# A fused attention and MLP block with its backward pass: k and v projected first with late q tiles, a deeper skew in attention backward, and reordered weight-gradient stages

One core of a Trainium2 chip. The metric is the device time of one execution in microseconds (us).

## The reference

Sequence 2048, width 640, 32 heads of 20, MLP width 1728, bfloat16. Forward: a layer norm, linear attention and a residual, then a layer norm, a gated MLP and a residual. The kernel returns the output and the gradients of x and of the five weights.

```python
def _A_ref(x, wqkv, wo):                     # linear attention
    q, k, v = ...                            # x @ wqkv, split into heads
    phi = lambda t: jnp.where(t > 0, t + 1, jnp.exp(t)) + 1e-6
    pq, pk = phi(q), phi(k)
    kv = jnp.einsum("bhsd,bhse->bhde", pk, v)
    z = jnp.einsum("bhsd->bhd", pk)
    num = jnp.einsum("bhqd,bhde->bhqe", pq, kv)
    den = jnp.einsum("bhqd,bhd->bhq", pq, z)[..., None] + 1e-6
    return merge(num / den) @ wo             # "merge" stands for the transpose and reshape

def _B_ref(x, w1, w3, w2):
    return (_silu(x @ w1) * (x @ w3)) @ w2   # written with einsum in the original

h = x + _A_ref(_layernorm(x), A_wqkv, A_wo)
h2 = h + _B_ref(_layernorm(h), B_w1, B_w3, B_w2)
# outputs: h2, and jax.vjp's gradients of x, wqkv, wo, w1, w3, w2 for grad_out
```

All q tiles need only x. But num and den need the sum of pk and v over the whole sequence, so no attention output can begin before the last k and v tile.

## The kernel before

Rows are cut into 16 tiles of 128 (`ST`) and four chunks of four tiles (`SC`, `TPC`); `part()` below issues the next nine of a turn's 54 ghn matmuls (or a piece of the gradient of wo, once those are done). `T`, `V`, `A`, `G` are TensorE, VectorE, ScalarE and GpSimd. In the traces shown here each engine's work comes in the order in which this program lists it. The stages, in order:

1. Projection: for every tile q, then k, then v.

```python
for t in range(ST):
    q = p1_mm(t, 0)                       # ten 320-column matmuls
    if t + 2 < ST:
        p1_norm(t + 2)
    phi(q, pqc[g][:, i, :])
    if t + 1 < ST:
        p1_tr(t + 1)
    k = p1_mm(t, D)
    phi(k, pkc[g][:, i, :])
    v = p1_mm(t, 2 * D)
    A.copy(...)                           # v to va
    ...                                   # statistics, kv_group once per four tiles, stores, loads
```

2. The first four attention outputs, as a chain of steps per tile: `f2_nd` (numerator and denominator), `f2_o` (division), `f2_ot` (transpose), `f2_at` (times wo, plus the residual), `f2_hn` (norm), `f2_ht` (transpose). Products of w2 for the MLP's backward (`filler`) fill TensorE between the steps.

3. Four MLP chunks of 14 column blocks. Per block: the ghh product (backward, with w2; in the first chunk the filler has made it before), gate and up products on TensorE, activations on ScalarE, seven elementwise operations on VectorE. The attention steps of the next chunk ("side steps") come after a whole block:

```python
for fc in range(FT):
    mlp(c, fc, ghh0[:, fc, :] if c == 0 else None)   # gate, up, then 7 elementwise operations
    if o2:
        next(o2)                                     # output products of the chunk before
    if c + 1 < SC:
        for f, i in sorted(side.get(fc, ()), key=lambda x: x[1]):
            f((c + 1) * TPC + i)
```

4. The last output products, the gradient of w2 (its operand hb is hh loaded transposed; grad_out is loaded after the fourth chunk).

5. Attention backward, one turn per tile. The layer-norm backward is one piece, and gnd (the gradient of num and den) is made and transposed within one turn:

```python
def ln_bwd(acc, t, nrm, st, out, res, pl):
    A.activation(out=gs, in_=acc, ..., accum_out=s[:, 0:1])
    V.scalar_tensor_tensor(out=wb[:], ...)
    V.tensor_scalar(...); V.tensor_scalar(...)
    V.scalar_tensor_tensor(out=wb[:], ...)
    A.activation(out=y[:], in_=wb[:], ...)            # waits for VectorE's wb
    V.tensor_tensor(out=out, in0=y[:], in1=res, op=ALU.add)   # out is g_h, waits for ScalarE's y

for t in range(ST + 2):
    g = b_ghn(t) if t < ST else wog       # 54 matmuls in six parts, then b_ln
    u = t - 2
    ...
    part()
    if u >= 0:
        b_go(u)                           # ten matmuls (h), then gnd on VectorE
    part()
    part()
    if u >= 0:
        b_gndT(u)                         # six transposes of gnd
    part()
    if u >= 0:
        b_gkv(u)
        b_gpq(u)
    part()
    if 0 <= t - 1 < ST:
        b_gT(t - 1)                       # transposes of g_h, copy ghT on ScalarE
    part()
```

6. The k and v backward with w1 and w3 gradient products ("jobs", from the transposed block gb) as filler, the x-gradient loop with the rest of them, and last the gradient of wqkv.

Of the kernel before, what the change touches and what calls it, by code (L numbers as in the profile page):

```python
# [8 lines left out]
P = 128  # L9
# [53 lines left out]
def kernel(  # L63
# [86 lines left out]

    p1 = pool("p1", "right")
    ps = pool("p1p", space=PSUM)
    wqkv = p1.tile([P, DT, 3 * D], BF16, name="wqkv")
    wq_v = A_wqkv.rearrange("(c p) n -> p c n", p=P)
    dma(out=wqkv[:, :, 0:D], in_=wq_v[:, :, 0:D])
    dma(out=x_sb[:, 2:4, :], in_=xS[:, 2:4, :])
    dma(out=wqkv[:, :, D:2 * D], in_=wq_v[:, :, D:2 * D])
    dma(out=wqkv[:, :, 2 * D:], in_=wq_v[:, :, 2 * D:])
    for t in range(4, ST, 4):
        dma(out=x_sb[:, t:t + 4, :], in_=xS[:, t:t + 4, :])  # L160
# [3 lines left out]
    def make_mask():  # L164
# [8 lines left out]
        G.memset(kvbd[:], 0.0)  # L173
# [4 lines left out]
    w2 = U1.tile([P, FT, D], BF16, name="w2", tag="D")  # L178
# [18 lines left out]
    pkc, pqc = {}, {}  # L197
    xnT, xns = {}, {}
# [5 lines left out]
    def p1_tr(t):  # L204
        xn = xns.pop(t)
        tr = ps.tile([P, DT, P], BF16, name="tr", bufs=2)
        for c in range(DT):
            T.transpose(tr[:, c, :], xn[:, c * P:(c + 1) * P], ident[:])
        xnT[t] = p1.tile([P, DT, P], BF16, name="xnT", bufs=2)
        A.copy(out=xnT[t][:], in_=tr[:])  # L210

    def p1_mm(t, n0):
        acc = ps.tile([P, 2, 512], F32, name="big", bufs=3)
        for j in range(2):
            for c in range(DT):
                T.matmul(acc[:, j, 0:HD], lhsT=xnT[t][:, c, :],  # L216
                         rhs=wqkv[:, c, n0 + j * HD:n0 + (j + 1) * HD], start=(c == 0), stop=(c == DT - 1))
        return acc

    def phi(acc, dst):  # L220
        mq = p1.tile([P, D], BF16, name="mq", bufs=3)
        A.activation(mq[:].rearrange("p (j n) -> p j n", j=2), acc[:, :, 0:HD], AF.Exp)
        V.tensor_scalar(out=mq[:], in0=mq[:], scalar1=1.0, scalar2=1e-6, op0=ALU.min, op1=ALU.add)
        V.scalar_tensor_tensor(out=dst.rearrange("p (j n) -> p j n", j=2), in0=acc[:, :, 0:HD], scalar=0.0,  # L224
                               in1=mq[:].rearrange("p (j n) -> p j n", j=2), op0=ALU.max, op1=ALU.add)
# [43 lines left out]
    for t in range(ST):  # L269
        g, i = divmod(t, TPC)  # L270
        if i == 0:
            pqc[g] = p1.tile([P, TPC, D], BF16, name="pqc", bufs=2)
            pkc[g] = p1.tile([P, TPC, D], BF16, name="pkc", bufs=2)
        q = p1_mm(t, 0)
        if t + 2 < ST:
            p1_norm(t + 2)
        phi(q, pqc[g][:, i, :])
        if t + 1 < ST:
            p1_tr(t + 1)
        k = p1_mm(t, D)  # L280
        phi(k, pkc[g][:, i, :])
        v = p1_mm(t, 2 * D)
        A.copy(out=va[g % 2][:, i, 0:C].rearrange("p (j h e) -> p j h e", j=2, e=DA)[:, :, :, 0:DH],
               in_=v[:, :, 0:HD].rearrange("p j (h e) -> p j h e", e=DH))
        if t % 2 == 0 and t + 4 < ST:
# [3 lines left out]
        if i == TPC - 1:  # L289
            sl = slice(g * TPC, (g + 1) * TPC)  # L290
            dma(out=pq_v[:, sl, :], in_=pqc[g][:])
            dma(out=pk_v[:, sl, :], in_=pkc[g][:])
            dma(out=va_v[:, sl, :], in_=va[g % 2][:])
            if g < 2:
                load_pqT(g)
# [4 lines left out]
    p1.release()  # L300
# [4 lines left out]
    pa = pool("pa", "right")  # L305
# [10 lines left out]
    def f2_o(t):  # L316
        o_t = pa.tile([P, D], BF16, name="o_t", bufs=2)
        den = pa.tile([P, H], F32, name="den", bufs=2)
# [12 lines left out]
    def f2_ot(t):  # L331
# [3 lines left out]
        oT[t] = pa.tile([P, DT, P], BF16, name="oT", bufs=2)  # L335
        A.copy(out=oT[t][:], in_=tr[:])

    def f2_at(t, tag="nd"):
        for j in range(2):
            at = ps.tile([P, 512], F32, name="at", tag=tag, bufs=2)  # L340
            for c in range(DT):
                T.matmul(at[:, 0:HD], lhsT=oT[t][:, c, :], rhs=wo[:, c, j * HD:(j + 1) * HD],  # L342
                         start=(c == 0), stop=(c == DT - 1))
            xs = x_sb[:, t, j * HD:(j + 1) * HD]
            V.tensor_tensor(out=xs, in0=at[:, 0:HD], in1=xs, op=ALU.add)
        ln2.run(x_sb, t, t + 1)

    def f2_hn(t):
        hn[t] = pa.tile([P, D], BF16, name="hn", bufs=2)
# [3 lines left out]
    def f2_ht(t):  # L353
        c, i = divmod(t, TPC)
        if i == 0:
            hnT[c] = pa.tile([P, DT, W], BF16, name="hnT", bufs=2)
# [15 lines left out]
    def mlp(c, fc, ghh):  # L372
        if ghh is None:
            ghp = mm5(w2T, fc, g2T[c])
            ghh = ew("ghh")
            A.copy(out=ghh[:], in_=ghp[:])  # L376
            ghh = ghh[:]
# [4 lines left out]
        A.copy(out=gate[:], in_=gp[:])  # L382
        upp = mm5(w3, fc, hnT[c])
# [8 lines left out]
        V.tensor_tensor(out=gate[:], in0=gate[:], in1=ghh, op=ALU.mult)  # L392
        dma(out=gg_d[F + f0:F + f0 + n, cs], in_=gate[:n, :])
        V.tensor_tensor(out=sig[:], in0=sig[:], in1=up[:], op=ALU.mult)
        V.tensor_tensor(out=sig[:], in0=sig[:], in1=ghh, op=ALU.mult)
        dma(out=gg_d[f0:f0 + n, cs], in_=sig[:n, :])

    def o2_steps(c, q=dma):
# [3 lines left out]
        for n, (i, j, fc) in enumerate(jobs):  # L402
            if fc == 0:
                o2["ps"] = ps.tile([P, 512], F32, name="o2", bufs=2)
                if j == 0:
                    o2["sb"] = pa.tile([P, D], BF16, name="h2", bufs=3)
# [11 lines left out]

    ghh0 = pa.tile([P, FT, W], BF16, name="hhT", bufs=2)
    fill = list(range(FT))  # L420

    def filler(n):
        for _ in range(n):
            if fill:
                fc = fill.pop(0)
                acc = mm5(w2T, fc, g2T[0])
                A.copy(out=ghh0[:, fc, :], in_=acc[:])

# [7 lines left out]
    for step in (2, (f2_ndo, 0), 2, (f2_ot, 0), (f2_ndo, 1), 1, (f2_at0, 0), 1, (f2_ot, 1), (f2_ndo, 2), 1,  # L436
                 (f2_hn, 0), (f2_at0, 1), 1, (f2_ht, 0), (f2_ot, 2), (f2_ndo, 3), 1, (f2_hn, 1), (f2_at0, 2), 1,
                 (f2_ht, 1), (f2_ot, 3), 1, (f2_hn, 2), (f2_at0, 3), 2, (f2_ht, 2), (f2_hn, 3), 1, (f2_ht, 3)):
        if isinstance(step, int):
            filler(step)  # L440
        else:
            step[0](step[1])
    filler(len(fill))

    V.memset(w2[64:, FT - 1, :], 0.0)
    side = {}
    for i in range(TPC):
        for k, fs in ((3 * i, (f2_nd, f2_o)), (3 * i + 1, (f2_ot,)), (3 * i + 2, (f2_at,)),
                      (3 * i + 3, (f2_hn,)), (3 * i + 4, (f2_ht,))):
            side.setdefault(k, []).extend((f, i) for f in fs)  # L450

    for c in range(SC):
        hhT[c] = pa.tile([P, FT, W], BF16, name="hhT", bufs=2)
        o2 = o2_steps(c - 1) if c > 0 else None
        for fc in range(FT):
            mlp(c, fc, ghh0[:, fc, :] if c == 0 else None)
            if o2:
                next(o2)
            if c + 1 < SC:
                for f, i in sorted(side.get(fc, ()), key=lambda x: x[1]):  # L460
                    f((c + 1) * TPC + i)
# [5 lines left out]
            if fc == 5 and c + 2 < SC:  # L467
                load_pqT(c + 2)


    g2 = U1.tile([P, ST, D], BF16, name="g2", tag="Q")
    dma(out=g2[:], in_=goS)
# [10 lines left out]
    pa.release()  # L483
    ps.release()
# [6 lines left out]
    woT = U1.tile([P, DT, D], BF16, name="woT", tag="W6")  # L491
    tail = br.tile([P, DT, P], BF16, name="w13tail")

    def load_w13():
# [4 lines left out]
        dmaT(out=woT[:], in_=A_wo[:, :])  # L499
# [13 lines left out]
    for fc in range(FT):  # L513
# [14 lines left out]
        if fc == 7:  # L528
            load_gg(0)
            load_gg(1)  # L530
# [34 lines left out]
    hnb, pqb, ghT, gnd, gndT = {}, {}, {}, {}, {}  # L565

    def b_load(t):
# [3 lines left out]
        pqb[t] = br.tile([P, D], BF16, name="pqb", bufs=4)  # L571
# [17 lines left out]
    def ln_bwd(acc, t, nrm, st, out, res, pl):  # L589
# [12 lines left out]
        y = pl.tile([P, D], BF16, name="y")  # L602
        A.activation(out=y[:], in_=wb[:], func=AF.Identity, bias=s[:, 3:4], scale=st.rs[:, t:t + 1])  # L603
        V.tensor_tensor(out=out, in0=y[:], in1=res, op=ALU.add)

    def b_ln(acc, t):
        ln_bwd(acc, t, hnb[t][:], ln2, g_h[:, t, :], g2[:, t, :], br)
# [8 lines left out]
    gnd_s = [br.tile([P, CP], BF16, name=f"gnd{i}") for i in range(3)]  # L616
# [3 lines left out]
    def b_go(t):  # L620
        gnd[t] = gnd_s[t % 3]
# [44 lines left out]
    def wo_job(m):  # L666
        acc = ps.tile([P, 2, 512], F32, name="gwo", tag="ghn", bufs=2)
        for j in range(2):
            for t in range(ST):
                T.matmul(acc[:, j, 0:HD], lhsT=o_sb[:, t, m * P:(m + 1) * P], rhs=g_h[:, t, j * HD:(j + 1) * HD],  # L670
                         start=(t == 0), stop=(t == ST - 1))
                if t % 8 == 7:
                    yield
# [11 lines left out]
    for t in range(ST + 2):  # L685
# [4 lines left out]
        u = t - 2  # L690
        if t + 2 < ST:
            b_load(t + 2)
# [214 lines left out]
```

## Time and profile before

| | before |
|---|---|
| time, median (range) | 1003.67 us (999.65 to 1006.38), 3 runs |
| span of the profiled run | 1005.6 us |
| TensorE busy / idle | 902.2 / 103.4 us |
| mean granted clock | 0.976 |

The prediction shows the page's head and the waits. What follows is another cut of the same run, by stage, with borders at the same instruction in both kernels (within 0.2 us), so that the rows can be set against those of the changed kernel. They are: the last projection work to the first gate product; the first chunk; the last output products and the w2 gradient; attention backward; the rest. Columns are window, length, busy us of TensorE, its weight loads, VectorE, ScalarE and GpSimd (instructions in brackets), granted clock, DMA share, GB/s.

```profile
88.05:119.89 31.84, 26.57 (x196) 15.66 (x194) 19.33 (x57) 13.97 (x24) 2.21 (x4) 1.00 0.31 108
119.89:181.07 61.18, 47.55 (x245) 23.07 (x245) 51.07 (x141) 34.94 (x64) 2.58 (x4) 0.89 0.53 159
391.01:480.99 89.98, 78.12 (x564) 55.50 (x564) 5.14 (x15) 10.53 (x16) 0.00 (x0) 0.94 1.09 249
480.99:697.11 216.12, 187.77 (x1553) 136.68 (x1553) 93.53 (x216) 54.30 (x85) 0.00 (x0) 0.98 0.44 112
697.11:1005.60 308.49, 280.49 (x2381) 214.74 (x2380) 66.47 (x166) 103.07 (x203) 0.00 (x0) 0.98 0.50 113
```

Read a row as length minus TensorE's busy time, which is its idle time, and then look at the clock: work done below 1.00 is stretched but counts as busy. The backward row has 28.35 us of idle; the first chunk 13.63 and a clock of 0.89.

### The profile page before, as it was taken

Reading aid. Unit: us, or ns where it says so; the run is one execution under the profiler, and the core shown is the slowest. Engines: PE = TensorE matmul, PEld = TensorE weight load, DVE = VectorE, ACT = ScalarE, POOL = GpSimd, SP = SyncE. Lnnn points to the kernel's source line nnn. Section 1 sums busy time; section 2 is a strip of 40 time slices with the busy share of each in tenths; the row PEclk is TensorE's granted clock in tenths of the full one; section 3 lists DMA queues with packets and bytes.
Section 4 is the critical chain, followed back from the end, with each engine's and each line's share of the span. In section 5 each row is a group of like instructions: output and inputs, shape, how many; then the busy total and the mean of one; then the engine's idle time right before and its main releaser. Section 6 shows DMA issues by size and latency. Waiting matters only on the chain.

```text
span 1005.6 us, 16837 instructions
## 1 busy us (share of the span) xinstructions
PE 902.2 (90%) x6741; PEld 614.0 (61%) x6741; DVE 458.2 (46%) x1162; ACT 383.0 (38%) x682; POOL 24.5 (2%) x43
## 2 busy tenths in 40 slices
PE   5999888899999999699888888889899898888998
PEld 4776443455555556476656666667687666666776
DVE  6875688787778765000244444442122123343000
ACT  3554545555665662011222222221122245554111
POOL 4000000000000000000000000000000000000000
PEclk9999988999999999799999999999899999999999
DMA  9794174252242326999244444329999943211111
GB/s 277 217 272 162 45 227 139 90 165 89 92 144 99 99 93 188 244 215 281 85 111 111 110 111 110 98 94 223 189 213 234 208 109 97 59 46 41 39 40 37
DMA packets 272541, 138.31 MB, mean 138 GB/s; under 512 B 173904, under 2 KB 271184, under 8 KB 272464
## 3 DMA queue, kind: packets, MB, share of 16 engines
q1 hardware_dynamic: 253952, 124.05, 48.7%
q10 hardware_dynamic: 18512, 13.20, 4.3%
q8 instruction: 52, 0.85, 0.4%
q14 instruction: 25, 0.20, 0.1%
HBM read 45.20 MB, written 50.02 MB: 95 GB/s over the span
## 4 chain that ended last, share of the span: by engine, by line
PE 62%; DVE 15%; ACT 8%; DMA 8%; SPq 3%; issue 2%; ACTq 1%; POOL 0%; DVEq 0%
PE mm L365 16%; PE job L756 16%; PE ghn L582 7%; PE o L407 5%; PE big L216 4%; PE gxn L843 3%; ACT y L603 2%; DVE wb L596 2%; DMA hb<-hh_d 2%; PE gw L519 2%; DVE wb L601 2%; ACT gs L593 2%; PE at L342 2%; PE gwo L670 2%; DMA ggb<-gg_d 2%
## 5 line engine op out<-in xcount | busy, mean ns | idle before, releaser
L365 PE MATMUL mm<-hnT,w 128*128 128x512 bf16 x560 | 135.5, 391 | 0.9 <-ACT hnT L360 0.9
L756 PE MATMUL job<-gb,hnN 128*128 128x288 bf16 x960 | 127.9, 288 | 7.1 <-DMA gb<-gg_d 5.0
L756 PEld LDWEIGHTS <-hnN 128*128 128x128 bf16 x960 | 92.5, 98 | 30.9 <-DMA gb<-gg_d 5.2
L582 PEld LDWEIGHTS <-ggb 128*128 128x128 bf16 x864 | 82.9, 98 | 31.0 <-issue 0.5
L365 PEld LDWEIGHTS <-w 128*128 128x128 bf16 x560 | 56.1, 101 | 68.6 <-issue 8.4
L760 ACT CAST obs<-job 128x288 bf16<-128x288 f32 (+1 forms) x90 | 36.6, 407 | 136.2 <-PE job L756 113.3
L843 PE MATMUL gxn<-wqT,gT 128*128 128x320 bf16 x480 | 76.1, 303 | 5.5 <-DMA wqT<-in_A_wqkv_dram 5.5
L216 PE MATMUL big<-wqkv,xnT 128*128 128x320 bf16 x480 | 71.4, 306 | 4.5 <-DVE pqc L224 2.8
L519 PE MATMUL gw<-g,hb 128*128 128x320 bf16 (+1 forms) x448 | 63.3, 305 | 8.0 <-DMA hb<-hh_d 8.0
L365 PE MATMUL mm<-g2T,w2T 128*128 128x512 bf16 x280 | 69.9, 382 | 0.0
L582 PE MATMUL ghn<-w13a,ggb 128*128 128x320 bf16 x448 | 69.7, 304 | 0.0
L407 PE MATMUL o<-w,hhT 128*128 128x320 bf16 x448 | 67.9, 299 | 1.0 <-DVE h L412 1.0
L582 PE MATMUL ghn<-w13b,ggb 128*128 128x320 bf16 x416 | 63.8, 299 | 0.0
L216 PEld LDWEIGHTS <-xnT 128*128 128x128 bf16 x480 | 47.2, 100 | 23.5 <-issue 4.5
L519 PEld LDWEIGHTS <-hb 128*128 128x128 bf16 (+1 forms) x448 | 44.9, 101 | 26.4 <-DMA hb<-hh_d 8.3
L407 PEld LDWEIGHTS <-hhT 128*128 128x128 bf16 x448 | 43.8, 98 | 24.9 <-issue 1.2
L843 PEld LDWEIGHTS <-gT 128*128 128x128 bf16 x480 | 45.6, 99 | 21.1 <-DMA wqT<-in_A_wqkv_dram 5.8
L756 PEld LDWEIGHTS <-xnN 128*128 128x128 bf16 x480 | 47.0, 98 | 18.2
L603 ACT ACTIVATE y<-wb,s,ln_rs 128x640 bf16<-128x640 f32 x32 | 29.4, 920 | 65.8 <-DVE wb L601 65.8
L387 DVE TENSOR_TENSOR gate<-gate,sig 128x512 bf16<-128x512 bf16 x56 | 23.7, 423 | 53.8 <-ACT gate L382 53.6
L376 ACT CAST ghh<-mm 128x512 bf16<-128x512 f32 x42 | 24.6, 585 | 57.8 <-issue 51.0
L380 ACT ACTIVATE sig<-mm 128x512 bf16<-128x512 f32 x56 | 33.4, 597 | 34.4 <-PE mm L365 33.4
(131 smaller groups left out, 1190.8 us busy)
## 6 DMA issues: line engine op xcount, KB each, us to landing
ggb<-gg_d SPq DMA_DIRECT2D x8, 1728.0 KB, 9.0
hh_d<-hhT SPq DMA_DIRECT2D x52, 128.0 KB, 1.8
gg_d<-gate SPq DMA_DIRECT2D x52, 128.0 KB, 1.9
gg_d<-sig SPq DMA_DIRECT2D x52, 128.0 KB, 1.8
out_dram<-obs ACTq DMA_DIRECT2D x60, 72.0 KB, 3.3
w<-in_B_w_dram SPq DMA_DIRECT2D x4, 864.0 KB, 6.6
va_d<-va SPq DMA_DIRECT2D x4, 768.0 KB, 6.8
out_dram<-gw2o ACTq DMA_DIRECT2D x18, 160.0 KB, 6.0
```

The costliest lines, as they stand in the source:

```text
L216: T.matmul(acc[:, j, 0:HD], lhsT=xnT[t][:, c, :], rhs=wqkv[:, c, n0 + j * HD:n0 + (j + 1) * HD], start=(c == 0), stop=(c == DT - 1))
L365: T.matmul(acc[:], lhsT=w[:, c, fc * P:(fc + 1) * P], rhs=rhs[:, c, :], start=(c == 0), stop=(c == DT - 1))
L376: A.copy(out=ghh[:], in_=ghp[:])
L380: A.activation(sig[:], gp[:], AF.Sigmoid)
L387: V.tensor_tensor(out=gate[:], in0=gate[:], in1=sig[:], op=ALU.mult)
L407: T.matmul(o2["ps"][:, 0:HD], lhsT=hhT[c][:, fc, i * P:(i + 1) * P], rhs=w2[:, fc, j * HD:(j + 1) * HD], start=(fc == 0), stop=(fc == FT - 1))
L519: T.matmul(acc[:n, j, 0:HD], lhsT=hb[b][:, t, i * P:i * P + n], rhs=g2[:, t, j * HD:(j + 1) * HD], start=(t == 0), stop=(t == ST - 1))
L582: T.matmul(acc[:, j, 0:HD], lhsT=ggb[t // 2][:, k, lo:lo + P], rhs=rhs[:, j * HD:(j + 1) * HD], start=(k == 0), stop=(k == NG - 1))
L603: A.activation(out=y[:], in_=wb[:], func=AF.Identity, bias=s[:, 3:4], scale=st.rs[:, t:t + 1])
L756: T.matmul(acc[:, 0:n], lhsT=lhs[:, t, m * P:(m + 1) * P], rhs=rhs(t), start=(t == 0), stop=(t == ST - 1))
L760: A.copy(out=ob, in_=acc[:, 0:n])
L843: T.matmul(acc[:, j, 0:HD], lhsT=gT[t][:, k, :], rhs=wqT[:, k, j * HD:(j + 1) * HD], start=(k == 0), stop=(k == 14))
```

## The change

It touches five places. (a) Front: k and v come first, and the q tiles of the first half are projected four tiles later in the same loop; the other eight ("late q") replace the ghh filler between the first attention outputs. Those ghh products go into the first chunk. For the first eight tiles the residual is added on TensorE (a matmul with the identity) and ScalarE evicts. VectorE, not GpSimd, clears kvbd. (b) Some side steps move between the gate and the up product. (c) grad_out and woT are loaded during the fourth chunk. (d) Attention backward: gnd is used one turn later, and the second half of `ln_bwd` is put off. (e) The filler of the k and v backward becomes q-gradient products, which need no transposed load; the w1 and w3 gradients go to the end; wqT is loaded early, x normalised early; one of three gT copies goes to VectorE.

The core of the diff (cut: pools and buffers, renamed loads, helper functions):

```diff
@@ projection
-        q = p1_mm(t, 0)
+        k = p1_mm(t, D)
         if t + 2 < ST:
             p1_norm(t + 2)
-        phi(q, pqc[g][:, i, :])
+        phi(k, pkc[g][:, i, :])
...
-        k = p1_mm(t, D)
-        phi(k, pkc[g][:, i, :])
         v = p1_mm(t, 2 * D)
...
+        if 4 <= t < 12:
+            q_tile(t - 4)
@@ make_mask
-        G.memset(kvbd[:], 0.0)
+        V.memset(kvbd[:], 0.0)
@@ f2_at
+            if on_pe:                                   # t < 8
+                T.matmul(at[:, 0:HD], lhsT=ident[:], rhs=xs, start=True, stop=False)
...
+            if on_pe:
+                A.copy(out=xs, in_=at[:, 0:HD])
+            else:
+                V.tensor_tensor(out=xs, in0=at[:, 0:HD], in1=xs, op=ALU.add)
@@ MLP
         A.copy(out=gate[:], in_=gp[:])
+        between()                                       # run_side(0, fc)
         upp = mm5(w3, fc, hnT[c])
...
+        for k, pos, f in ((3 * i, 0, f2_ndo), (3 * i + 1, 1, f2_ot), (3 * i + 2, 1, f2_at), (3 * i + 3, 0, f2_hn),
+                          (3 * i + 4, 0, f2_ht)):
+            side[pos].setdefault(k, []).append((f, i))
...
+            if c == SC - 1 and fc == 0:
+                g2 = U1.tile([P, ST, D], BF16, name="g2", tag="Q")
+                for i in range(SC):
+                    dma(out=g2[:, i * TPC:(i + 1) * TPC, :], in_=goS[:, i * TPC:(i + 1) * TPC, :])
@@ ln_bwd
-        y = pl.tile([P, D], BF16, name="y")
-        A.activation(out=y[:], in_=wb[:], func=AF.Identity, bias=s[:, 3:4], scale=st.rs[:, t:t + 1])
-        V.tensor_tensor(out=out, in0=y[:], in1=res, op=ALU.add)
+        def rest():
+            ...                                         # the same three lines
+        return rest
@@ attention backward
-    for t in range(ST + 2):
+    for t in range(ST + 3):
...
+        u, w = t - 2, t - 3
...
+        if 0 <= u < ST:
+            b_gT(u)
...
         part()
+        if w >= 0:
+            b_gndT(w)
+            b_gkv(w)
+        part()
+        if 0 <= u < ST:
             b_go(u)
         part()
+        if t - 1 in ln_rest and t < ST:
+            ln_rest.pop(t - 1)()
         part()
+        if w >= 0:
+            b_gpq(w)
@@ k and v backward, x gradient, end
-    jobs = w13_jobs()
+    jobs = wq_jobs((0,))
...
+        if i % 2:
+            next(jobs, None)
...
+        if t == 7:
+            wqT = U1.tile([P, 15, D], BF16, name="wqT", tag="D")
+            dmaT(out=wqT[:], in_=A_wqkv[:, :])
...
+        if k == 1:
+            V.tensor_copy(out=gT[t][:, k * DT:(k + 1) * DT, :], in_=tr[:])
+        else:
+            A.copy(out=gT[t][:, k * DT:(k + 1) * DT, :], in_=tr[:])
...
+    for i, (_, out, f0) in enumerate(blocks):
+        load_block(i + 2)
+        for m in range(DT):
+            grad_job(hnN, m, lambda t: gb[i][:, t, :], NB, out[:, m, f0:f0 + NB])
```

## The prediction

> **What bounds the kernel now.** I read the page first, then the table of stretches by stage, then TensorE's waits, then the timeline where those waits are long.
>
> ```profile
> span 1005.6 us, 16837 instructions
> PE 902.2 (90%) x6741; PEld 614.0 (61%) x6741; DVE 458.2 (46%) x1162; ACT 383.0 (38%) x682; POOL 24.5 (2%) x43
> PEclk9999988999999999799999999999899999999999
> ```
>
> TensorE bounds the whole and no other engine is near it: 103.4 us of the 1005.6 are idle on it. The digits of 7 and 8 in the clock row are a second loss, matmuls run at a lower clock. The change removes no matmul, so all it can win is idle time and clock. Where they lie, by stage (columns: window, length, busy us of PE, PEld, DVE, ACT, POOL, then clock, DMA share, GB/s):
>
> ```profile
> 0.00:22.40 22.40, 12.27 (x75) 8.22 (x76) 15.06 (x41) 7.34 (x10) 11.54 (x22) 1.00 0.99 275
> 120.00:181.00 61.00, 47.37 (x245) 22.97 (x244) 51.00 (x141) 34.83 (x64) 2.58 (x4) 0.89 0.53 159
> 391.00:412.00 21.00, 13.47 (x98) 9.48 (x97) 3.80 (x8) 0.00 (x0) 0.00 (x0) 0.87 1.10 274
> 481.00:670.00 189.00, 162.38 (x1357) 118.51 (x1357) 83.48 (x195) 49.25 (x78) 0.00 (x0) 0.99 0.35 95
> 697.00:717.00 20.00, 14.99 (x117) 11.27 (x116) 1.89 (x7) 3.16 (x7) 0.00 (x0) 0.84 1.16 226
> 806.00:925.00 119.00, 107.09 (x913) 80.48 (x911) 44.27 (x112) 60.85 (x105) 0.00 (x0) 0.99 0.26 68
> ```
>
> So the idle is: start 10.1, first MLP chunk 13.6, before the w2 gradient 7.5, attention-backward loop 26.6, entry to the k/v backward 5.0, the x-gradient loop 11.9. What ends it (TensorE's waits; total, count, longest):
>
> ```profile
> PE h1b L641 <- DVE gnd L636: 27.2, 15, 1.9
> PE trq L836 <- ACT gT L837: 10.3, 14, 1.6
> PE tr L334 <- ACT hnT L360: 9.0, 11, 1.0
> PE tr L359 <- DVE hn L145: 8.4, 4, 3.1
> PE gw L519 <- DMA hb<-hh_d: 8.0, 1, 8.0
> PE gxn L843 <- DMA wqT<-in_A_wqkv_dram: 5.5, 1, 5.5
> PE job L756 <- DMA gb<-gg_d: 5.0, 1, 5.0
> ```
>
> These are exactly the places that the diff touches. What a wait costs afterwards, from the timeline: sixteen 288-column matmuls after the 5 us wait, and the same sixteen when nothing preceded them:
>
> ```profile
> 713.10 4.02 PE L756 MATMUL job<-gb,hnN 128*128 128x288 bf16 x16 [5.01 <-DMA gb<-gg_d]
> 717.42 2.12 PE L756 MATMUL job<-gb,hnN 128*128 128x288 bf16 x16
> ```
>
> **What the Trainium skill says.** "TensorE: Matmul & The Clock Gate", Part 1: the array runs at half rate when cold and after an idle window of about 3.4 us, and needs as long a busy stretch to recover. The trace agrees: 4.02 against 2.12 us above. "Perfetto Trace Analysis", Tensor Engine Instruction: VectorE and ScalarE are strict FIFO, and TensorE only pulls weight loads ahead; so moving an instruction in program order alone can remove a wait. The trace shows the wait: the transposes of gnd sit two parts behind the product they depend on, and every later ghn matmul stands behind them. "SBUF — State Buffer", two separate sides: VectorE and GpSimd share an exclusively locked port pair. At 17.7 us GpSimd clears kvbd in 3.30 us, and beside it a 128x2 VectorE operation takes 2.48 us instead of 0.17: agreed. "DMA: Bandwidth & Descriptors", Issuing engines are not separate DMA queues: all transfers share 16 engines. The share of 1.10 in the window before the w2 gradient, where the 2.56 MB of grad_out and the transposed load of hh run together, fits.
>
> **Part by part.** Full-rate costs from the chain of work: ten 320-column matmuls 1.36 us, fifteen 512-column ones 3.24, sixteen 288-column ones 1.97. Nearly all matmuls stay; added are 16 residual matmuls by the identity, 16 x 0.136 = 2.2 us.
>
> (a) Front, 0 to 181 us (start of the second MLP chunk). Removed from projection: eight of sixteen q tiles, 8 x 1.36 = 10.9 us. Its start gets worse: x tiles 2 and 3 now come behind all of wv (0.8 MB, about 3 us at 275 GB/s), and VectorE clears kvbd itself (a memset of this size takes 1.66 us in L715) in front of the norm of tile 2. I put that norm at 18.5 us instead of 14.0, and TensorE's idle time in the start at 15 instead of 10. Projection then ends near 82 instead of 89.5. Next the eight late q tiles take the place of the 14 ghh products as filler between the first attention outputs: 10.9 + 4 x 3.0 (nd, two transposes, output product) + 2.2 = 25 us of TensorE. ScalarE pays 4 x 0.43 per late tile (two exponentials, two relus of 320 columns), 13.8 in all, plus 9.0 for attention; 22.8 beside 25, so it trails closely. Following the three FIFOs by hand I find some 6 us of waits, so the first gate product at 114 instead of 119.9. In the first chunk the ghh products now fill TensorE: 12 x 3.24 + 2 x 2.16 + 12.1 = 55.3 us, against VectorE 14 x 7 x 0.424 + 4 x 3.24 = 54.5 (four tiles' residual adds, 0.97 each, went to ScalarE) and ScalarE 50. Three engines within 10%: I take 58.5, so it ends at 172.5. **Saving 8.5.**
>
> (b) Chunks two and three: hn, its transpose and nd move between gate and up products, so the single transpose bank has 2 us between its two users. Idle there is 72.0 - 69.7 and 71.0 - 68.7. **Saving 4** of 4.7. The fourth chunk is 62.00 busy of 62.00: nothing.
>
> (c) w2 gradient: grad_out and woT are loaded in the fourth chunk, where the DMA share is 0.31. hb (11.5 us to landing by the DMA view, some of it queueing) then lands near 403, when the last output matmuls end (404.5). Gone: the 8.0 us wait and its cold clock (the first 128 gw matmuls took 19.7 us, full rate is 17.4). Without woT in the queue (4.58 us of issue at 457) ggb arrives before it is needed, and the 3.3 us wait for kvbdT behind the crowded queues goes. **Saving 13.5.**
>
> (d) Attention backward: the period per tile is 12.03 us, of which TensorE idles 1.87: the chain gs, wb, y, g_h stands in VectorE's queue before gnd. The skew gives gnd a whole period, and the second half of the layer norm is put behind gnd. 14 x 1.87 = 26.2. The bound becomes TensorE at 10.2 per tile; VectorE needs 6.1 and ScalarE 3.3. Drain and entry: idle 1.7 and cold clock (0.94 over 27 us) partly go; one more, shorter turn, same matmuls. **Saving 29.**
>
> (e) From 697 to the end: idle is 5.0 + 2.1 + 5.5 + 11.9 + 3.9 = 28.4, and about 6 of cold clock (1 minus clock times length). New: q-gradient products need nothing from DRAM but x, loaded 20 us ahead, so the gb wait goes; wqT is asked for midway in the k/v stage, so the 5.5 goes; one of three gT copies goes to VectorE and xnN is ready, so the 10.3 mostly goes. Against it: the k/v stage loses most filler (60 products become 10). Per pair of tiles TensorE has 2 x 1.02 + 2.18 = 4.2 us; in the tile without a product the next nd waits for ScalarE's two g_v copies (0.47 + 0.43 against 0.5 of other work), 0.6 x 8 = 5. Four loads of transposed k and v (7.6 us issue each, plus 2.4 for pk) against 8.4 us of compute per group: some 3. Entry: VectorE norms eight x tiles (3.5), clears and masks gkv_b (3.2): 3 of wait. Remaining: x-gradient loop 3, tail 3.3, cold clock 2, unforeseen 2: 21 in place of 34. **Saving 13.**
>
> Sum 8.5 + 4 + 13.5 + 29 + 13 = 68; 1003.7 - 68 = 936.
>
> **Rivals.** First: the front gains nothing. For it: ScalarE's relus, late x tiles, three engines nearly level in chunk one. Against it: 19 us idle and a 0.89 clock lie in 88 to 181 now. It makes the time 943. Second: DMA becomes the bound, through the k/v stage's loads, or because grad_out (11 us of transfer) delays the hh and gg stores of the fourth chunk, whose tiles have three buffers of 4.3 us each. For it: these stages run at a share of 1.0 and more today. Against it: the filler's transposed gb loads (8.4 us each) leave the k/v stage. It costs 10 to 20: 946 to 956. Third: the skew only moves the wait from gnd to another small bank user, since six allocations per turn share two h1 banks. For it: the same banks. Against it: each has a ghn part (1.23 us) between, and evictions take 0.5 to 0.8. It would leave 10 of the 29: 946. Fourth, the good one: waits nearly vanish and only start and tail (18 us) stay: 1005.6 - 85 - 20 + 2, roughly 915.
>
> **Range and chances.** The backward loop and the w2 gradient (42) are well supported; front and tail are where I guessed queues. One rival true adds 7 to 20, luck takes off up to 20: 918 to 958. Slower would need all of it lost elsewhere. Faster by 2% 0.97, within 0.025, slower 0.005.
>
> **What would show it.** Right: L641's successor waits less than 3 us in total and the backward period is 10.2 to 10.5; no TensorE wait on hb above 1 us; first gate product near 114 and second chunk near 172; TensorE idle about 40 to 50 in all. Wrong: TensorE waits on q's activations or on pk, vaT loads of over 8 us; stores of hh or gg waiting in the fourth chunk; a start idling more than 20 us. A time above 958 would mean that the k/v stage or the front became bound by ScalarE or DMA.

## The result and the profile after

The changed kernel takes 919.50 us (median of 4 runs, 918.74 to 919.95); the kernel before took 1004.09 in the same comparison (4 runs, 999.65 to 1006.38). The ratio is 0.9162, with a 95% interval of 0.9129 to 0.9194. Ratios here are the mean time of one kernel's fast runs over that of the other's of the same rounds, so not quite the ratio of the medians. All outputs are right. The time lies in the predicted range of 918 to 958, but near its lower end, 16.5 us below the predicted 936: more was won than the prediction thought.

The head of the page of the changed kernel, in the same form as the prediction shows for the one before:

```profile
span 917.3 us, 16861 instructions
PE 883.4 (96%) x6729; PEld 611.5 (67%) x6757; DVE 449.0 (49%) x1146; ACT 388.7 (42%) x722; POOL 22.5 (2%) x42
PEclk9999999999999999999999999999999999999999
```

TensorE's idle time went from 103.4 to 33.9 us. Its busy time fell by 18.8, although matmuls were added: no slice shows a lowered clock any more, and the mean clock is 0.998. A rough size for that, an estimate from the records: one minus the clock, times the span, is 24 us before (0.024 x 1005.6) and 2 after. So the change won in two currencies, about 70 us of waiting and about 20 of slow clock, and I read the second as brought by the first, since nothing was done for the clock as such; no run separates the two. The runs also spread less, 1 us against 7.

The same five stages of the changed kernel:

```profile
77.99:108.28 30.29, 25.81 (x223) 18.25 (x222) 21.59 (x65) 22.01 (x52) 2.21 (x4) 1.00 0.61 205
108.28:164.76 56.48, 53.50 (x307) 27.87 (x313) 47.28 (x130) 43.59 (x83) 2.20 (x4) 1.00 0.59 173
367.90:446.68 78.78, 76.15 (x565) 54.75 (x565) 5.17 (x14) 10.53 (x16) 0.00 (x0) 1.00 1.09 245
446.68:628.94 182.26, 181.48 (x1552) 136.30 (x1551) 97.10 (x225) 52.57 (x85) 0.00 (x0) 1.00 0.44 122
628.94:917.30 288.36, 279.38 (x2382) 214.95 (x2379) 64.22 (x156) 98.72 (x203) 0.00 (x0) 0.99 0.55 127
```

From these borders the gain by stage, predicted and measured:

| part | predicted | measured | from |
|---|---|---|---|
| (a) projection | 7.5 | 10.1 | its last kv products start at 77.99, were 88.05 |
| (a) to the first gate product | -1.6 | 1.6 | 30.29 against 31.84 long |
| (a) first chunk | 2.7 | 4.7 | 56.48 against 61.18 |
| (b) chunks two to four | 4 | 6.8 | 203.14 against 209.94 |
| (c) w2 gradient | 13.5 | 11.2 | 78.78 against 89.98 |
| (d) attention backward | 29 | 33.9 | 182.26 against 216.12 |
| (e) to the end | 13 | 20.1 | 288.36 against 308.49 |
| sum | 68 | 88.3 | |

The backward stage has 0.78 us of idle left in 182. What TensorE still waits for in the changed kernel (total, count, longest):

```profile
PE tr L213 <- DVE xn L145: 9.3, 3, 6.0
PE tr L349 <- ACT hnT L395: 4.2, 5, 0.9
PE dkv L702 <- DMA vaT<-va_d: 2.2, 1, 2.2
PE gw L559 <- DMA hb<-hh_d: 1.3, 1, 1.3
PE dkv L847 <- DMA pkT<-pk_d: 1.2, 1, 1.2
```

The 27.2 us for gnd, the 10.3 for ScalarE's gT, the 8.0 for hb (1.3 left), the 5.5 for wqT and the 5.0 for gb are gone or nearly so, and no wait of their size stands where they stood. The largest wait now is the first norm of x, at the very start.

The first chunk took in twelve ghh products, about 13 us of TensorE (12 x 1.08, from one product to the next in the timeline), and yet got 4.7 us shorter: its idle time fell from 13.63 to 2.98 us, and its clock rose from 0.89 to 1.00. The next two fences show where a norm of the next chunk (hn) stands in VectorE's queue in that chunk; columns are start, duration, engine and line, operation, and in brackets the idle time before it with its releaser. The kernel before:

```profile
138.88 0.43 DVE L395 TENSOR_TENSOR sig<-sig,hhT 128x512 bf16<-128x512 bf16 x1
139.22 0.44 DVE L145 TENSOR_SCALAR hn<-x_sb,ln_mv,ln_rs 128x640 bf16<-128x640 bf16 x1
139.72 0.45 PE L359 MATMUL tr<-ident,hn 128*128 128x128 bf16 x5 [1.97 <-DVE hn L145]
```

And the changed kernel:

```profile
122.00 0.45 DVE L145 TENSOR_SCALAR hn<-x_sb,ln_mv,ln_rs 128x640 bf16<-128x640 bf16 x1 [0.66 <-POOL ln_rs L142]
123.84 0.44 PE L394 MATMUL tr<-ident,hn 128*128 128x128 bf16 x5
123.84 0.41 DVE L428 TENSOR_TENSOR gate<-gate,sig 128x512 bf16<-128x512 bf16 x1
```

Before, hn starts behind the last of the seven elementwise operations of the block, and TensorE waits 1.97 us for it. After, hn goes ahead of the first of them (L428), and the transposes have no wait.

### The profile page after: what moved, and what is told of

It is laid out like the page before. It is cut to its first block, busy times and chain, and to the rows that moved or that the text cites. A ratio compares the mean times of both kernels' runs of the same rounds, so it can differ in the third digit from the quotient of the medians.

```text
span 917.3 us, 16861 instructions
## 1 busy us (share of the span) xinstructions
PE 883.4 (96%) x6729; PEld 611.5 (67%) x6757; DVE 449.0 (49%) x1146; ACT 388.7 (42%) x722; POOL 22.5 (2%) x42
## 4 chain that ended last, share of the span: by engine, by line
PE 82%; DVE 2%; DMA 2%; ACT 2%; issue 1%; ACTq 0%; DVEq 0%
PE job L796 20%; PE mm L400 19%; PE ghn L625 13%; PE gxn L897 7%; PE gw L559 7%; PE o L448 5%; PE h L675 2%; PE at L361 2%; PE gwo L716 2%; DMA hb<-hh_d 2%; PE trq L887 1%; DMA vaT<-va_d 1%; PE dkv L702 1%; PE h L702 1%; PE h1b L687 1%
## 5 line engine op out<-in xcount | busy, mean ns | idle before, releaser
L400 PE MATMUL mm<-hnT,w 128*128 128x512 bf16 x546 | 132.7, 379 | 1.7 <-ACT hnT L395 1.0
L796 PE MATMUL job<-gb,hnN 128*128 128x288 bf16 x960 | 117.8, 286 | 0.0
L400 PEld LDWEIGHTS <-w 128*128 128x128 bf16 x560 | 53.8, 98 | 61.3 <-issue 1.1
L625 PE MATMUL ghn<-w13a,ggb 128*128 128x320 bf16 x448 | 67.8, 299 | 0.0
L559 PE MATMUL gw<-g,hb 128*128 128x320 bf16 (+1 forms) x448 | 61.1, 299 | 1.3 <-DMA hb<-hh_d 1.3
L219 PE MATMUL big<-wqkv,pqT 128*128 128x320 bf16 x400 | 59.6, 305 | 2.7 <-DVE kvacc L258 1.0
L625 PE MATMUL ghn<-w13b,ggb 128*128 128x320 bf16 x416 | 61.2, 299 | 0.0
L448 PEld LDWEIGHTS <-hhT 128*128 128x128 bf16 x448 | 43.8, 98 | 24.9 <-issue 1.2
L219 PEld LDWEIGHTS <-pqT 128*128 128x128 bf16 x480 | 46.4, 99 | 20.8 <-DVE kvacc L258 1.3
L412 ACT CAST ghh<-mm 128x512 bf16<-128x512 f32 x56 | 32.9, 588 | 63.3 <-issue 39.3
L796 PEld LDWEIGHTS <-xnN 128*128 128x128 bf16 x480 | 47.2, 99 | 18.5
L636 ACT ACTIVATE gs<-ghn 128x640 bf16<-128x640 f32 x16 | 11.3, 705 | 95.8 <-PE ghn L625 95.8
```

Of the source, the lines that this page charges most:

```text
L219: T.matmul(acc, lhsT=pqT[:, c, t * P:(t + 1) * P], rhs=wqkv[:, c, n0:n0 + HD], start=(c == 0), stop=(c == DT - 1))
L400: T.matmul(acc[:], lhsT=w[:, c, fc * P:(fc + 1) * P], rhs=rhs[:, c, :], start=(c == 0), stop=(c == DT - 1))
L412: A.copy(out=ghh[fc][:], in_=acc[:])
L448: T.matmul(o2["ps"][:, 0:HD], lhsT=hhT[c][:, fc, i * P:(i + 1) * P], rhs=w2[:, fc, j * HD:(j + 1) * HD], start=(fc == 0), stop=(fc == FT - 1))
L559: T.matmul(acc[:n, j, 0:HD], lhsT=hb[b][:, t, i * P:i * P + n], rhs=g2[:, t, j * HD:(j + 1) * HD], start=(t == 0), stop=(t == ST - 1))
L625: T.matmul(acc[:, j, 0:HD], lhsT=ggb[t // 2][:, k, lo:lo + P], rhs=rhs[:, j * HD:(j + 1) * HD], start=(k == 0), stop=(k == NG - 1))
```

## Experiments

Each edit is against the changed kernel (919.50 us, and 919.43 as a control); "cost" is the median minus that. The kernel before measured 1004.55 to 1005.79 beside them. The first four runs each undo one part, to see whether the gain of a stage in the trace is the worth of that part.

### a_old: the front of the kernel before, with the early loads kept

Undone: k and v first, late q, residual on TensorE, kvbd on VectorE, ghh in the first chunk, and the place of the side steps, so (a) and (b) together. Core of the edit:

```diff
-        k = p1_mm(t, D)
+        q = p1_mm(t, 0)
...
-        if 4 <= t < 12:
-            q_tile(t - 4)
...
-            mlp(c, fc, lambda: run_side(0, fc))
+            mlp(c, fc, ghh0[:, fc, :] if c == 0 else None)
...
```

> The changed kernel with the front of the kernel before (q, k and v together, ghh products as filler, no residual on TensorE), the early loads of grad_out and woT kept. Theory (the stages' savings are independent): the front up to the last output products came 23.1 us earlier in the changed kernel than in the kernel before, so this run should be 919.5 + 23 = 942 us, and the first gate product should start at 119 to 120 us and the second chunk near 181. Rival (part of the front's gain was only brought forward and is given back where the later stages wait on transfers): 925 to 933 us.

Measured: 944.40 us (942.26 to 945.47, 4 runs), ratio to the kernel before 0.9387 (0.9352 to 0.9422), clock 0.987. The cost is 24.9, near the 23.1 that the stages of (a) and (b) gave (10.1 + 1.6 + 4.7 + 6.8, rounded). The first gate product is at 122.79, and TensorE's 9.0 us of waits for hn are back. So the front is worth about 25 us: the rival that it gains little falls.

### c_late: grad_out and woT loaded where they were

```diff
-            if c == SC - 1 and fc == 0:
-                g2 = U1.tile(...)
-                ...                       # and woT at fc == 4
+    g2 = U1.tile([P, ST, D], BF16, name="g2", tag="Q")
+    dma(out=g2[:], in_=goS)
...
+        dmaT(out=woT[:], in_=A_wo[:, :])
```

> The changed kernel with grad_out loaded in front of the first hh block and woT after the w1, w3 transposes, as in the kernel before. Theory: TensorE waits 8 us for hb again, runs its first gw products cold and meets the kvbdT wait of 3 us; 919.5 + 11 = 930 us, hb landing some 10 us later. Rival (hb was always bound by its own transfer behind the last hh stores, and the fourth chunk only has less to do): less than 4 us slower, 923 us.

Measured: 934.10 us (931.78 to 935.50, 4 runs), ratio 0.9285 (0.925 to 0.932); cost 14.6. Both waits named in the prediction came back, by this kernel's list of TensorE's waits:

```profile
PE gw L556 <- DMA hb<-hh_d: 7.6, 1, 7.6
PE h1b L592 <- ACT kvbdT L595: 3.6, 2, 3.2
```

The waits add up to 11.2, of which the changed kernel has 1.3 for hb and 0.8 for kvbdT too. By the table's borders the stage takes 89.38 us (369.00 to 458.38, clock 0.96) in place of 78.78 (clock 1.00): 10.6 us of the cost lie in it, near the 11.2 of the table, and 1.8 in attention backward behind it.

### d_noskew: the old order in attention backward

The old loop (two tiles of lag), and the second half of `ln_bwd` at once. One impurity: the 16 norms of x that the new loop has in its extra turns stand behind the loop here, 5.79 us of VectorE.

```diff
-        ln_rest[t] = ln_bwd(acc, t, hnb[t][:], ln2, g_h[:, t, :], g2[:, t, :], br)
+        ln_bwd(acc, t, hnb[t][:], ln2, g_h[:, t, :], g2[:, t, :], br)()
...
-    for t in range(ST + 3):
+    for t in range(ST + 2):
...                                       # b_go, b_gndT, b_gkv, b_gpq, b_gT as before
+    for j in range(ST):
+        ln1.norm(xnN[:, j, :], xnN[:, j, :], j)
```

> The changed kernel with the attention backward in the old order (two tiles of lag, second half of the layer norm at once). Theory: period per tile back from 10.0 to 12.0 us, TensorE waiting about 1.87 us per tile on gnd, 919.5 + 28 to 31 = 948 to 951 us. Rival (the gain came from the lower load of a better filled clock and from the later start of loads, not from the order): under 935 us.

Measured: 952.81 us (952.22 to 954.25, 4 runs), ratio 0.9471 (0.9433 to 0.951); cost 33.3, the largest of the four. The one wait that accounts for most of it:

```profile
PE h1b L687 <- DVE gnd L682: 28.7, 15, 2.2
```

### e_old: the stages after attention backward as before

```diff
-    jobs = wq_jobs((0,))
+    jobs = w13_jobs()
...
-        if k == 1:
-            V.tensor_copy(out=gT[t][:, k * DT:(k + 1) * DT, :], in_=tr[:])
-        else:
-            A.copy(out=gT[t][:, k * DT:(k + 1) * DT, :], in_=tr[:])
+        A.copy(out=gT[t][:, k * DT:(k + 1) * DT, :], in_=tr[:])
...                                       # wqT, norms of x and the order of the stages too
```

> The changed kernel with everything after the attention backward as in the kernel before (w1 and w3 gradients beside the k and v stage, qkv gradients last, wqT late). Theory: the waits for gb (5), wqT (5.5), gT (10) and the cold matmuls behind them come back; 919.5 + 20 = 940 us. Rival (my on-record step: the new k and v stage loses most of it again, so the parts are worth 13): 932 us.

Measured: 943.00 us (938.00 to 945.58, 4 runs), ratio 0.937 (0.9327 to 0.9413); cost 23.5. Two of the waits that came back:

```profile
PE trq L888 <- ACT gT L889: 10.5, 14, 1.6
PE job L808 <- DMA gb<-gg_d: 4.4, 2, 3.0
```

With 5.2 us for wqT they make 20.1, the size of this stage's measured gain. The prediction's 13 was too small: it had set new waits against this gain.

The four costs sum to 96.3 against a whole gain of 84.6 (1004.09 - 919.50). They don't add up exactly. The norms behind the loop in d_noskew and spells of slow clock, which differ from run to run, are candidates; what the 12 us are stays open.

### a_noqlate: no late q tiles

All q tiles in the projection, nothing in their place between the attention outputs. It asks what the late tiles are worth.

```diff
-        if 4 <= t < 12:
+        if t >= 4:
             q_tile(t - 4)
+        if t >= 12:
+            q_tile(t)
...
-    for f, t in ((q_late, 8), (q_late, 9), (f2_ndo, 0), (q_late, 10), ...
+    for f, t in ((f2_ndo, 0), (f2_ot, 0), (f2_ndo, 1), ...
```

> The changed kernel, but all sixteen q tiles in the projection stage and no late ones: the first attention outputs then run without any filler, while the ghh products stay inside the first chunk. Theory (the late tiles are worth what they fill): projection ends 11 us later, the stage between it and the first gate product shrinks from 29 to about 22 us because its chain of VectorE and ScalarE work stays, so 4 to 8 us slower, 924 to 928 us, with TensorE waits of over 6 us more on o_t, oT and hn. Rival (the front's gain is all from the ghh products in the first chunk): 919 to 921 us. Other rival (nothing of the 11 us is hidden): 930 us.

Measured: 933.54 us (931.75 to 934.21, 4 runs), ratio 0.9284 (0.9246 to 0.9322); cost 14.0. I expected less; the rival in which nothing of the filler was hidden by other work came nearest. Eight q tiles are 10.9 us of TensorE by the prediction's step, and the last kv products moved by 11.1 (from 77.99 to 89.05). I had expected the stage behind to shrink to about 22 us. It took 31.7 from there to the first gate product, against 30.3 with the late tiles and 31.8 in the kernel before with its ghh filler. But this run doesn't show how long the stage needs without filler, because a wait of another kind came into it. From its timeline:

```profile
106.00 0.89 DVE L343 TENSOR_TENSOR o_t<-nd,rden 128x380 bf16<-128x380 f32 x2 [4.95 <-DMA o_d<-o_t]
```

VectorE stood idle for 4.95 us until the store of an earlier o_t had left its buffer (there are two). That store was issued only at 100.95, behind two transposed loads of pqT (91.78 and 97.02); the changed kernel has one such load here, at 90.50. TensorE did nothing from 102 to 107, and from 107 to 111 its clock was 0.50. So the late tiles are worth 14.0 us in this program. Whether the stage without them would come to 22 us if the stores were not held up stays open.

### a_resV: the residual on VectorE again

```diff
-        on_pe = t < 2 * TPC
+        on_pe = False
```

> The changed kernel with the residual added by VectorE for all tiles, none by TensorE with ScalarE copies: TensorE has 2.2 us less, VectorE 8 times 0.97 us more. Theory (the first chunk is bound by TensorE alone, VectorE has the queue to hide it): 917 to 920 us. Rival (VectorE is level with TensorE there, my step on record): 4 us slower, 923 us.

Measured: 923.55 us (920.97 to 925.07, 6 runs), ratio 0.9179 (0.9151 to 0.9207); cost 4.1. The rival's number held and my theory missed, but the rival's reason, a nearly full VectorE in the first chunk, covers only part: the stage ahead of that chunk takes 32.4 us in place of 30.3, in the changed kernel and in the control alike, and the chunk 57.9 in place of 56.5. So 2.1 us lie ahead of the chunk and 1.4 in it. As this run was on another chip than the control, with intervals that overlap, the total of 4 is not clear of noise by itself.

### a_kvbdG: kvbd cleared by GpSimd again

```diff
-        V.memset(kvbd[:], 0.0)
+        G.memset(kvbd[:], 0.0)
```

> The changed kernel with kvbd cleared by GpSimd again. Theory on record (clearing it on VectorE costs 1.7 us in front of the norm of tile 2, but the GpSimd version locks VectorE out for 2.3 us some 3 us later): the two nearly cancel, 918 to 921 us. Rival (the shared port is the larger cost, as VectorE is the tight engine there): 2 us or more slower.

Measured: 923.63 us (922.50 to 924.41, 6 runs), ratio 0.9182 (0.9157 to 0.9207); cost 4.1, and TensorE's waits for the norms of x rise from 9.3 to 11.0. The prediction had listed the move to VectorE as something that makes the start worse. This run says the opposite: the sign was wrong. The trace shows where the time goes. While GpSimd clears kvbd (18.71, 3.30 us), the 128x2 VectorE operation at 18.45 takes 3.58 us (0.17 in the changed kernel), and TensorE waits 3.97 us for the norm behind it, where the changed kernel waits 2.56 and 0.75. None of these six runs overlaps with the nine of the changed kernel and the control (918.68 to 920.92), but the control was on another chip and the intervals of the ratios overlap, so the trace is the stronger evidence here.

### b_side: all side steps behind the output products again

```diff
-        for k, pos, f in ((3 * i, 0, f2_ndo), (3 * i + 1, 1, f2_ot), (3 * i + 2, 1, f2_at), (3 * i + 3, 0, f2_hn),
-                          (3 * i + 4, 0, f2_ht)):
+        for k, pos, f in ((3 * i, 1, f2_ndo), (3 * i + 1, 1, f2_ot), (3 * i + 2, 1, f2_at), (3 * i + 3, 1, f2_hn),
+                          (3 * i + 4, 1, f2_ht)):
```

> The changed kernel with all side steps of the chunks (nd and o, hn and its transpose) behind the output products again instead of between gate and up. Theory: the waits of tr on hnT (0.8 to 0.9 each) and of the hn transpose on the norm come back in the first three chunks; 4 us of my second part plus some of the first chunk, 6 to 9 us slower than the control. Rival (only the ghh products fill the chunks): within 2 us of the control.

Measured: 933.16 us (930.57 to 933.86, 5 runs), ratio 0.9276 (0.9252 to 0.93); cost 13.7 where I expected 6 to 9. The first chunk takes 63.06 us (110.17 to 173.23) in place of 56.48, and the other three 208.41 in place of 203.14. The waits of this kernel, to be set against 4.2 for the first and 0.9 each for the other two in the changed kernel:

```profile
PE tr L349 <- ACT hnT L395: 8.9, 11, 0.9
PE tr L349 <- DVE o_t L341: 3.1, 2, 2.2
PE tr L394 <- DVE hn L145: 2.5, 7, 0.7
```

So moving a few instructions by half a block, with no change of work, is worth 6.6 us in the first chunk and 5.3 in the others. The 6.6 are more than the 4.7 that the first chunk gained: with the ghh products in it and the old places it would have been longer than before.

### d_rest_now: the extra tile of lag without the deferred half

The new order stays; only the second half of `ln_bwd` is done at once.

```diff
-        ln_rest[t] = ln_bwd(acc, t, hnb[t][:], ln2, g_h[:, t, :], g2[:, t, :], br)
+        ln_bwd(acc, t, hnb[t][:], ln2, g_h[:, t, :], g2[:, t, :], br)()
...
-        if t == ST:
-            ln_rest.pop(t - 1)()
```

> The changed kernel with the extra tile of lag kept but the second half of the layer norm issued at once, so in front of gnd in VectorE's queue. Theory (the extra tile alone removes the wait, gnd has a whole period): 919 to 922 us. Rival (the order in VectorE's queue is what removes it): 1 us per tile, 933 us or more.

Measured: 940.04 us (938.86 to 943.55, 6 runs), ratio 0.9355 (0.9322 to 0.9389); cost 20.5. I had held that the extra tile does the work and that the deferral hardly matters (919 to 922). That theory fell. The wait for gnd is indeed gone, but another one takes its place, in this kernel's list of waits:

```profile
PE h L675 <- ACT ghT L660: 17.2, 15, 1.8
```

Why, from the timeline of d_rest_now, one turn:

```profile
543.71 0.88 DVE L644 SCALAR_TENSOR_TENSOR wb<-hnb,s,gs 128x640 f32<-128x640 bf16 x1
544.71 0.92 ACT L648 ACTIVATE y<-wb,s,ln_rs 128x640 bf16<-128x640 f32 x1 [2.09 <-DVE wb L644]
545.54 0.67 ACT L660 COPY ghT<-h1b 128x640 bf16<-128x640 bf16 x1
```

The same turn of the changed kernel:

```profile
540.94 0.68 ACT L660 COPY ghT<-h1b 128x640 bf16<-128x640 bf16 x1
542.14 0.88 DVE L644 SCALAR_TENSOR_TENSOR wb<-hnb,s,gs 128x640 f32<-128x640 bf16 x1
543.14 0.92 ACT L648 ACTIVATE y<-wb,s,ln_rs 128x640 bf16<-128x640 f32 x1 [0.25 <-DVE wb L644]
```

In d_rest_now ScalarE stands idle for 2.09 us at y, which waits for VectorE's wb, and the copy ghT behind it, which doesn't need wb, comes only after y. TensorE needs ghT for h. In the changed kernel y is listed later, so ghT is copied before VectorE has made wb, and y itself has almost nothing left to wait for (0.25).

### d_defer: the deferred half without the extra tile of lag

The mirror image: the old order and lag, as in d_noskew (norms of x behind the loop too), but the second half of `ln_bwd` behind gnd.

```diff
-    for t in range(ST + 3):
+    for t in range(ST + 2):
...
         part()
-        if t - 1 in ln_rest and t < ST:
+        if t - 1 in ln_rest:
             ln_rest.pop(t - 1)()
...                                       # b_go, b_gndT, b_gkv, b_gpq, b_gT in the old order
```

> The attention backward in the old order with two tiles of lag, but with the second half of the layer norm issued behind gnd: the deferral without the extra tile. The wait on gnd was 1.87 us per tile; without y and the last add in front of it gnd is done about 1.5 us earlier. Theory (deferral and extra tile are two halves of one thing): period 10.4 to 10.6 us, 6 to 10 us slower than the control. Rival (the extra tile is what counts, since with the extra tile and no deferral 12.8 of 33 us were won): 20 us slower than the control, period 11.3 us.

Measured: 927.47 us (927.05 to 928.71, 5 runs), ratio 0.9225 (0.9202 to 0.9248); cost 8.0, as expected. TensorE's waits for gnd are 4.3 us over 14 turns, 0.3 at the longest, against 28.7 in d_noskew. With the two runs before it this gives a square:

| cost in us | half at once | half deferred |
|---|---|---|
| two tiles of lag | 33.3 (d_noskew) | 8.0 (d_defer) |
| three tiles of lag | 20.5 (d_rest_now) | 0 |

The deferral is worth 25.3 with the old lag and 20.5 with the new; the extra tile 12.8 and 8.0. Both are needed, and the half that the title of the change doesn't name is the larger.

### again and best2: a control, and a small step further

`again` is the changed kernel as it is.

> The changed kernel itself, unchanged, as the control on the same chip as the three others of this call. Theory: 918 to 921 us. Rival (the chips differ by some us, so the small differences of 4 us of the earlier call with the GpSimd memset and the residual add are not clear of that): 922 to 925 us.

Measured: 919.43 us (918.68 to 920.92, 5 runs), ratio 0.9147 (0.9123 to 0.917).

best2 clears kvbd and the pads before the statistics of x tiles 2 and 3, and asks for the transposed k and v ahead of pk:

```diff
-        V.memset(kvbd[:], 0.0)            # out of make_mask
...
-    ln1.run(x_sb, 2, 4)
     zero_pads()
+    V.memset(kvbd[:], 0.0)
+    ln1.run(x_sb, 2, 4)
     make_mask()
...
-            load_pk(c + 2)
             load_kT(c + 2)
+            load_pk(c + 2)
```

> The changed kernel with the memsets of the pads and of kvbd put on VectorE before the statistics of x tiles 2 and 3 (VectorE stands idle there from 6.8 to 10.0 us, they need 3.0), and in the k and v stage the transposed loads asked for before the plain pk load. Theory: the wait of 2.56 us for the norm of tile 2 and the one of 0.75 after it go, the loads' waits of 1.17 and 2.24 us and the cold product behind them (4.01 instead of 2.17) go in part; 3 to 6 us faster than the control in the same call. Rival (the start is bound by the arrival of x tiles 2 and 3 and VectorE catches up anyway; the loads wait for the buffers, not for their order): less than 1.5 us.

Measured: 916.95 us (914.93 to 920.46, 6 runs), ratio 0.9126 (0.9101 to 0.915). The waits named do what they should: 7.8 us for the norms in place of 9.3, and 0.2 in place of 3.4 for the two transposed loads. New ones stand beside them: 1.5 for ScalarE's gT and 0.8 for the weights of the projection. And the medians differ by 2.5 us and the intervals overlap with those of the control, so it isn't clear that it is faster.

## Why the prediction was right, and where its sizes were off

**What bounds the kernel.** Right: with TensorE 90% busy and no matmul removed, the gain had to be idle time and clock. Idle fell by 69.5 us. The prediction put the remaining idle at 40 to 50; it is 33.9.

**(a) Front, 8.5 predicted, 16.3 by the stages.** The mechanism was right. The step that failed is the start: a loss of 5 us was counted that did not come.

- The start. "I put that norm at 18.5 us instead of 14.0, and TensorE's idle time in the start at 15 instead of 10." The norm of tile 2 is at 16.28, and the idle time in the first 22.4 us is 10.1, as before (22.40 - 12.33). New waits of 2.56 and 0.75 us did come for later norms, but the wait of 1.8 us for the weights in the kernel before is gone (in this trace: four others with the new front have 1.1 to 1.6 of it). With the start no worse, nearly the whole 10.9 us of the eight removed q tiles is left as gain: 10.1. And a_kvbdG points to a gain from the memset on VectorE, which was counted as a loss. The sum itself slipped too: 10.9 won and 5 lost take the end of the projection from 89.5 to 83.6, not to 82.
- Between. "The first gate product at 114" came at 108.28. The end of the projection gives 2.5 us of this (79.5, predicted 82), and the stage 3.2 (28.8 us, where 82 to 114 had left 32). In it 25 us of TensorE and 6 of waits were predicted, 24.3 and 4.5 measured. The 25 held 1.1 too much: the 2.2 us for the residual on TensorE belong to eight tiles, and only four of them are here.
- The first chunk. "Three engines within 10%: I take 58.5"; it took 56.48, with TensorE busy for 53.50 where the sum had 55.3. The engines were not level: VectorE was busy for 47.28 and ScalarE for 43.59, not 54.5 and 50. The prediction named the new place of the side steps only for chunks two and three, under (b). b_side shows that this chunk needs it as well: without it, it takes 63.06.

**(b) 4 predicted, 6.8 measured.** The mechanism was right: b_side attributes 5.3 of it to the places. The prediction counted idle time alone. Idle time fell by 3.6 us (from 5.63 to 2.05), and TensorE's busy time by 3.2, as the clock rose from 0.99 to 1.00: the clock is the term that was left out.

**(c) 13.5 predicted, 11.2 by the stage, 14.6 by c_late (10.6 in this stage).** Right, with both waits: 7.6 us for hb and 3.6 for kvbdT come back when the loads are late. "No TensorE wait on hb above 1 us" was just missed, at 1.3 (0.6 in the control).

**(d) 29 predicted, 33.9 by the stage, 33.3 by d_noskew.** Right in its mechanism as written there: gnd gets a whole period, and the second half of the norm goes behind it. The period fell from 12.03 to 9.98 us, lower than the 10.2 predicted, and the drain gained too. While planning the experiments I gave the extra tile the whole credit; d_rest_now refuted that, and d_defer shows the deferral to be the larger half. The third rival, that the skew only moves the wait, is false for the whole change, but true for half of it: without the deferral 17.2 us of waits appear at ghT. They come from ScalarE's order, not from the banks that the rival named.

**(e) 13 predicted, 20.1 by the stage, 23.5 by e_old.** The removed waits were right. The new ones were overestimated: the prediction allowed 3 for the entry, 5 for evictions of g_v, 3 for loads of transposed k and v, 3 for the x-gradient loop. The changed trace shows 0.4 at the entry, 0.5 for evictions, 3.4 for the loads, 0.9 in the x-gradient loop. The loads alone were sized well.

**The rivals.** The front did gain (a_old). DMA did not become the bound: the w2 gradient's stage keeps its share of 1.09 and yet is 11.2 us shorter. The fourth, that waits nearly vanish and the time falls to 915, came nearest, at 919.5. The prediction used it only as the end of its range, and its sum holds a slip: 1005.6 - 85 - 20 + 2 is 902.6 and not 915, so that 915 came near is luck. Of the 20 us between 68 and 88, 7.8 lie in (a), 7.1 in (e), 4.9 in (d) and 2.8 in (b), and (c) takes back 2.3. The time is inside the range only because the range left 18 us below 936 for luck.

## What to carry to other kernels

When one engine bounds a kernel and the rest follow queues, list for each queue what stands in front of an instruction that the bound engine waits for: moving an instruction that itself waits for another engine to a later place can win more than another stage of lag (25 against 13 us here), and taking lag alone may only bring up the next entry of the queue. A stage in which the bound engine waits can take in work from another one: the first chunk took twelve products and got shorter, once its side steps stood in the right place. When you take filler out as a test, read the stage's waits before you call what is left its chain: in a_noqlate a delayed store stood in it. When you size such a change, do not set a new wait against each removed one by default, and count the spells of slow clock that short waits leave behind as part of the gain.

## What the Trainium skill lacked or had wrong

- "TensorE: Matmul & The Clock Gate", Part 1, ties the half rate to an idle window of about 3.4 us; its section on PSUM-queue depth-cycling adds that frequent short idles can do it too, but gives no length. In the timeline of d_noskew a single wait of 2.16 us for gnd, before which TensorE had run without a gap since the wait of the turn before, was followed by matmuls at about half rate; waits of 1.87 us in the neighbouring turns were not. The same eight matmuls after a wait of 1.87 us and after the one of 2.16:

```profile
483.05 1.25 PE L625 MATMUL ghn<-w13b,ggb 128*128 128x320 bf16 x8
495.47 2.34 PE L625 MATMUL ghn<-w13b,ggb 128*128 128x320 bf16 x8
```

- "SBUF — State Buffer", two separate sides, names the VectorE operations that take the shared ports: those in a two-port mode, or with two inputs from SBUF. In the changed kernel a GpSimd affine select that took 0.37 us elsewhere took 2.42 beside a VectorE memset of 1.66 us, which has no input at all. The same page, Who interferes with whom, has an operation with at most one such input not contend with GpSimd outside the two-port modes, and doesn't list a memset among those that have such a mode. Yet the select took 2.40 to 2.42 us in all ten runs with the memset in this place, and none with this shape took over 0.9 in best2 and a_kvbdG, where the memset is earlier or on GpSimd. The memset's mode isn't in the trace, so what holds the select up stays open.
- "Perfetto Trace Analysis", Tensor Engine Instruction, says that ScalarE is a strict FIFO, and the runs agree. No page that I read draws the consequence for an instruction that waits for another engine: it holds up evictions behind it that need nothing from that engine. Here that was 17.2 us of TensorE's time (d_rest_now), with a wait of 2.09 us per turn on ScalarE.
